# Issue in program order, with the stages written as a software pipeline, in a spectral filter and FFN kernel

## The chip, the cores and the metric

The kernel runs on one core of a Trainium2 chip. The metric is device time in microseconds, the median of three runs. The core has TensorE (PE, matmuls into PSUM), VectorE (DVE), ScalarE (ACT) and GpSimd (POOL) for elementwise work, and SyncE (SP), which issues the DMAs. Each engine takes its own instructions one after the other; semaphores make it wait for others.

## What is computed

```python
def reference(A_x, A_w_r, A_w_i, B_x, B_w1, B_b1, B_w2, B_b2):
    def _A_ref(x, w_r, w_i):
        B, S, D = x.shape
        X = (lambda x, axes=(-2,-1): jnp.fft.rfft2(x.astype(jnp.float32), axes=axes))(x, axes=(-2, -1))
        W = w_r + 1j * w_i
        X = X * W
        y = (lambda x, s, axes=(-2,-1): jnp.fft.irfft2(x, s=s, axes=axes).astype(jnp.bfloat16))(X, (S, D), axes=(-2, -1))
        return y
...
    x = A_x
    h = x + _A_ref(_layernorm(x, axis=-1), A_w_r, A_w_i)
    h2 = h + _B_ref(_layernorm(h, axis=-1), B_w1, B_b1, B_w2, B_b2)
    return h2
```

`x` is 2048 x 512 in bf16. The first half is a layernorm, a real 2-D FFT, a product with a complex filter, the inverse FFT and a residual. `_B_ref` is an FFN: 512 to 1792, the square of the ReLU, back to 512, with biases, on the layernorm of the result.

## The kernel before

The 2048 rows lie as 128 partitions of 16 groups `g`. Every FFT is written as matmuls with tables of sines, which the kernel makes itself: integer phases (`fiK`, `fiG`, `fiE`, `fiI`) on DVE or POOL, and the sine on ACT (`KF`, `GF`, `EF`, `GI`). `EI` and `KI` are transposes of EF and KF, made on PE and copied out by DVE.

The **front** loads `xs`, takes the statistics of each group (`bn_stats`, `bn_aggr` into `mv1`, then `rs1` on POOL), normalizes into `un`, and multiplies with KF (stage 1); ACT copies the result to `Bt`. Beside it the filter is scaled into `WB`: half of it straight on POOL, the reversed half through a matmul with a flip matrix `J` and a copy from PSUM (`pw`).

The **pair stage** is a loop `for pr in range(8)`. Stage 2 multiplies Bt by GF (8 matmuls of 256 columns, copy `U` on ACT). Stage 3 multiplies U by EF (4 of 512, copy `AB` on ACT, or `X` for pair 0). The spectral work on DVE makes `X` out of AB, the products `mA` and `mB` with WB, `Z` and `M`; POOL mends a few columns in `real_channels`. Stage 4 multiplies M by EI (8 of 256, copy into `T2` on ACT).

The **FFN part** works in chunks of four groups. `prep(c)` does stage 5 for each group (four matmuls of T2 with GI, copy `od` on ACT, sum and difference `R` on DVE), a matmul with KI, the residual `hs`, statistics, `hb` (hs with the last bias, on POOL), then `rs2`, the normalized `u2` and eight transposes twice into `UT`. `mlp(c)` does 14 times four matmuls of 512 columns with W1, a ReLU `rl` on ACT and its square `act` on DVE; then for each group 14 matmuls with W2 into `po`, the sum `ot` and the store.

The order of calls is `prep(0)`, `prep(1)`, `mlp(0)`, `prep(2)`, `mlp(1)`, `prep(3)`, `mlp(2)`, `mlp(3)`. The text does not fix the order in which an engine issues: the framework's scheduler orders each engine's instructions by its own priorities and cost figures, with the text's order as priority, and so mixes neighbouring steps where it finds them ready.

Of the kernel before, what the change touches and what calls it, by code (L numbers as in the profile page):

```python
# [19 lines left out]


@with_exitstack
def kernel(
# [127 lines left out]
    for c in range(4):  # L151
        for g in range(4 * c, 4 * c + 4):
# [3 lines left out]
        sl = slice(4 * c, 4 * c + 4)  # L156
        nc.gpsimd.tensor_scalar(rs1[:, sl], mv1[:, sl, 1], EPS, None, ALU.add)
        nc.gpsimd.tensor_tensor(rs1[:, sl], rs1[:, sl], mhalf[:], ALU.pow)  # L158
        for g in range(4 * c, 4 * c + 4):
            nc.vector.tensor_scalar(un[:, g, :], xs[:, g, :], mv1[:, g, 0:1], rs1[:, g:g + 1],  # L160
                                    ALU.subtract, ALU.mult)
        for h in range(2):
            pt = mm_tile("p1")
            pv = pt[:].rearrange("p (t e i c) -> p t e i c", t=2, e=2, i=2)
            g0 = 4 * c + 2 * h
            for t in range(2):
                for i in range(2):
                    g = g0 + i
                    o = pv[:, t, :, i, :]
                    nc.tensor.matmul(o, lhsT=un[:, g, P * t:P * t + P], rhs=KFlo, start=True, stop=False)  # L170
                    nc.tensor.matmul(o, lhsT=un[:, g, 256 + P * t:256 + P * t + P], rhs=KFhi, start=False, stop=True)
            dst = Bt[:].rearrange("p e q (g s) -> p e g q s", s=8)[:, :, g0:g0 + 2]
            nc.scalar.copy(dst, pt[:].rearrange("p (e i q s) -> p e i q s", e=4, i=2, q=16))

# [271 lines left out]
```

## Time and profile before

| | |
|---|---|
| median of three runs | 293.75 us (292.48 to 294.24) |
| profiled execution | 294.23 us |
| its span, first to last instruction | 292.4 us |
| mean granted TensorE clock | 0.784 |
| busy: PE, DVE, ACT, POOL | 180.6, 128.3, 93.0, 56.7 us |

The profile is one execution. Busy times are sums over the span; where engines take turns, no sum is near the span. The granted clock is 1.0 at the high level of 2.4 GHz and 0.5 at the low one of 1.2 GHz; a matmul's length follows it.

### The profile page before, as it was taken

What the parts mean: (1) busy time and instruction counts of PE and PEld (TensorE: products, weight loads), DVE (VectorE), ACT (ScalarE), POOL (GpSimd) and SP (SyncE); (2) the same over time, 40 slices, a digit from 0 to 9 for tenths busy, and PEclk for the clock granted to TensorE, in tenths of its full rate; (3) what the DMA queues carried; (4) which work ended last, traced back from release to release, by engine and by line L of the source; (5) the groups of instructions that cost most, each with busy time, mean ns of one, the idle gap of its engine ahead of it and who ended that gap; (6) DMA issues with size and microseconds to landing.
All of it is one profiled execution on the core that took longest, in us unless ns stands there. A gap on an engine that the chain in (4) does not pass through costs nothing.

```text
span 292.4 us, 2459 instructions
## 1 busy us (share of the span) xinstructions
PE 180.6 (62%) x858; PEld 93.2 (32%) x872; DVE 128.3 (44%) x299; ACT 93.0 (32%) x123; POOL 56.7 (19%) x109
## 2 busy tenths in 40 slices
PE   0066575363264245343536999329997449999995
PEld 0034364132133123121413444115443124444442
DVE  3795433224314413447572531753523744323421
ACT  1126661422341242121312830106700109505700
POOL 2776513101101110114332000340000430000000
PEclk9999576565775676555566999758999559999999
DMA  7994000000000000000000001000001000011011
GB/s 238 421 283 155 0 2 1 0 0 0 0 0 2 0 0 0 0 1 0 0 1 2 0 0 54 20 0 0 0 18 56 0 0 0 2 36 36 1 39 36
DMA packets 7469, 10.27 MB, mean 35 GB/s; under 512 B 2208, under 2 KB 6176, under 8 KB 7200
## 3 DMA queue, kind: packets, MB, share of 16 engines
q1 hardware_dynamic: 7456, 10.11, 10.2%
q8 instruction: 7, 0.11, 0.2%
q14 instruction: 6, 0.05, 0.1%
HBM read 8.01 MB, written 2.10 MB: 35 GB/s over the span
## 4 chain that ended last, share of the span: by engine, by line
PE 54%; DVE 26%; ACT 8%; POOL 5%; issue 3%; DMA 1%; POOLq 0%; ACTq 0%; DVEq 0%
PE ph L395 17%; PE po L403 16%; DVE hs L367 4%; PE p L251 3%; PE p L366 3%; DVE st L369 3%; DVE un L160 3%; ACT U L254 3%; DVE st L154 3%; PE p L385 3%; PE p L316 2%; ACT AB L277 2%; PE p L317 2%; DVE mA L288 2%; DVE R L363 2%
## 5 line engine op out<-in xcount | busy, mean ns | idle before, releaser
L395 PE MATMUL ph<-UT,W 128*128 128x512 bf16 x217 | 51.1, 387 | 0.3
L403 PE MATMUL po<-W,act 128*128 128x512 bf16 x220 | 48.8, 379 | 0.2
L397 ACT ACTIVATE rl<-ph,b1f 128x512 bf16<-128x512 f32 x56 | 37.2, 694 | 19.2 <-PE ph L395 18.8
L398 DVE TENSOR_TENSOR act<-rl 128x512 bf16<-128x512 bf16 x56 | 23.8, 425 | 33.0 <-ACT rl L397 33.0
L371 POOL TENSOR_TENSOR hb<-hs,b2b 128x512 f32<-128x512 bf16 x16 | 18.4, 1150 | 91.2 <-DVE hs L367 84.5
L316 PE MATMUL p<-EI,M 128*128 128x256 bf16 x28 | 11.6, 414 | 32.8 <-DVE M L300 32.8
L403 PEld LDWEIGHTS <-act 128*128 128x128 bf16 x224 | 22.0, 98 | 26.4
L395 PEld LDWEIGHTS <-W 128*128 128x128 bf16 x224 | 22.2, 100 | 24.7
L405 DVE TENSOR_TENSOR ot<-po,hb 128x512 bf16<-128x512 f32 x16 | 11.1, 692 | 35.5 <-PE po L403 35.5
L170 PE MATMUL p<-KF,un 128*128 128x256 bf16 x32 | 12.5, 395 | 20.1 <-DVE KF L127 14.2
L361 ACT COPY od<-p 128x256 f32<-128x256 f32 x16 | 6.0, 372 | 58.4 <-PE p L358 58.3
L282 DVE TENSOR_TENSOR X<-AB 128x512 bf16<-128x512 bf16 x7 | 3.0, 428 | 46.8 <-ACT AB L277 46.8
L366 PE MATMUL p<-R,KI 128*128 128x512 bf16 x16 | 8.9, 556 | 22.0 <-DVE R L364 22.0
L318 ACT CAST T<-p 128x1024 bf16<-128x1024 f32 x8 | 8.1, 1012 | 44.2 <-PE p L317 39.1
L385 PE MATMUL p<-ident,u 128*128 128x128 bf16 x64 | 9.5, 304 | 15.7 <-DVE u L378 15.2
L367 DVE TENSOR_TENSOR hs<-p,xs 128x512 bf16<-128x512 f32 x16 | 11.1, 692 | 10.4 <-PE p L366 10.4
L316 PEld LDWEIGHTS <-M 128*128 128x128 bf16 x28 | 3.6, 130 | 37.6 <-DVE M L300 36.7
L358 PE MATMUL p<-GI,T 128*128 128x256 bf16 x64 | 14.8, 373 | 1.1 <-ACT T L318 1.1
L386 ACT COPY UT<-p 128x1024 bf16<-128x1024 bf16 x8 | 7.7, 1015 | 24.2 <-PE p L385 24.2
L385 PEld LDWEIGHTS <-u 128*128 128x128 bf16 x64 | 7.3, 142 | 25.2 <-DVE u L378 22.4
L160 DVE TENSOR_SCALAR un<-xs,mv,rs 128x512 bf16<-128x512 bf16 x16 | 11.1, 742 | 4.7 <-POOL rs L158 4.7
L251 PE MATMUL p<-GF,Bt 128*128 128x256 bf16 x64 | 13.1, 370 | 0.0
(123 smaller groups left out, 241.2 us busy)
## 6 DMA issues: line engine op xcount, KB each, us to landing
W<-in_B_w_dram SPq DMA_DIRECT2D x2, 1792.0 KB, 12.7
xs<-in_A_x_dram SPq DMA_DIRECT2D x4, 512.0 KB, 5.6
out_dram<-ot SPq DMA_DIRECT2D x16, 128.0 KB, 1.8
Wn<-in_A_w_r_dram SPq DMA_DIRECT2D x1, 1028.0 KB, 9.1
Wn<-in_A_w_i_dram SPq DMA_DIRECT2D x1, 1028.0 KB, 10.8
b2b<-in_B_b_dram SPq DMA_DIRECT2D x1, 128.0 KB, 15.6
b1b<-in_B_b_dram SPq DMA_DIRECT2D x1, 3.5 KB, 15.9
```

The source lines that it names most:

```text
L160: nc.vector.tensor_scalar(un[:, g, :], xs[:, g, :], mv1[:, g, 0:1], rs1[:, g:g + 1], ALU.subtract, ALU.mult)
L251: nc.tensor.matmul(puv[:, q, :, e, :], lhsT=Bt[:, 2 * t + e, 2 * pr + q, :], rhs=GFv[:, t, :, e, :], start=(t == 0), stop=(t == 1))
L316: nc.tensor.matmul(o, lhsT=M[:, 0, r, c0:c0 + P], rhs=ei[:, P:3 * P], start=True, stop=False)
L358: nc.tensor.matmul(pe[:, 256 * e:256 * e + 256], lhsT=T2[:, lt, g].rearrange("p q s -> p (q s)"), rhs=GI[:, lt, :], start=(r == 0), stop=( ...
L366: nc.tensor.matmul(py[:], lhsT=KI[:], rhs=R[:], start=True, stop=True)
L367: nc.vector.tensor_tensor(hs[:, g, :], py[:], xs[:, g, :], ALU.add)
L371: nc.gpsimd.tensor_tensor(hb[:, g, :], hs[:, g, :], b2b[:], ALU.add)
L385: nc.tensor.transpose(pt[:, 512 * d + P * i:512 * d + P * i + P], u2[:, i, bass.ts(d2 + d, P)], ident[:])
L395: nc.tensor.matmul(ph[:], lhsT=W1[:, d, bass.ts(f, P)], rhs=UT[:, d, :], start=(d == 0), stop=(d == ND - 1))
L397: nc.scalar.activation(rl[:], ph[:], ACT.Relu, bias=b1f[:, f:f + 1], scale=1.0)
L398: nc.vector.tensor_tensor(act[:, f, :], rl[:], rl[:], ALU.mult)
L403: nc.tensor.matmul(po[:], lhsT=act[:, f, bass.ts(i, P)], rhs=W2[:, f, :], start=(f == 0), stop=(f == NF - 1))
```

## The change

Every engine's instructions are tied, each to the one before it, so that the engine issues in the order of the text (`pin`), and the text is written anew.

- In the front all phase tables come first, fiG on DVE instead of POOL. `xs` comes in five pieces. EF's third kind and EI's are negations of the first on DVE, so that 19 blocks are transposed instead of 28. Five of sixteen `un` go to ACT, two of the four WB copies to DVE. W2 is loaded ahead of the two biases.
- The pair loop is skewed: in one turn stage 4 of pair `pr - 1`, stage 3 of `pr + 1`, stage 2 of `pr + 2` and the spectral work of `pr`. U and AB have three buffers instead of two. The last T2 copy is split between ACT and DVE.
- The FFN works in chunks of 2, 2, 4, 4 and 4 groups. The next chunk's preparation is a list of steps (`prep_steps`, some of them empty), which `run` hands out between the slots of the current chunk: a slot is one W1 group, or some five W2 matmuls. `hb` follows `rs2` on POOL; half of the `u2` go to ACT and half of the UT copies to DVE. PSUM is split into three banks for preparation, three for `ph` and two for `po`.

```diff
+def pin(tc, nc):
+
+    last = {}
+    for ins in list(nc.cur_bb.bb.instructions):
+        prev = last.get(ins.engine)
+        if prev is not None:
+            tc.add_manual_dep(ins, prev.name,
+                              mybir.DependencyInfo(mybir.DependencyClass.NoSync, mybir.DependencyReason.DATA),
+                              reason="program order")
+        last[ins.engine] = ins
...
+    CH = ((0, 2), (2, 4), (4, 8), (8, 12), (12, 16))
+    for a, b in CH:
+        nc.sync.dma_start(xs[:, a:b, :], xv[:, a:b, :])
...
     nc.sync.dma_start(W1[:], B_w1.rearrange("(c p) f -> p c f", p=P))
+    nc.sync.dma_start(W2[:], B_w2.rearrange("(i p) d -> p i d", p=P))
     nc.sync.dma_start(b1b[:], B_b1.rearrange("(i p) -> p i", p=P))
     nc.sync.dma_start(b2b[:], B_b2.unsqueeze(0).to_broadcast([P, D]))
-    nc.sync.dma_start(W2[:], B_w2.rearrange("(i p) d -> p i d", p=P))
...
+        nc.vector.tensor_scalar(fiG[:, o:o + 257], idxL[:, 0:257], cols[:, t:t + 1], float(QT), ALU.mult, ALU.add)
...
+    for i, off in ((0, 0), (1, QT)):
+        nc.gpsimd.tensor_scalar(fiE[i][:], idxK[:], cols[:, 3:4], float(off), ALU.mult, ALU.add)
+        nc.scalar.activation(
+            EF[:, :, i, :], fiE[i][:].bitcast(I16)[:, ::2].rearrange("p (a b) -> p a b", a=9), ACT.Sin,
+            scale=SIN_SCALE)
...
+    ON_ACT = (3, 7, 11, 13, 15)
...
+    ln1_stats(0, 2)
+    nc.vector.tensor_scalar(EF[:, :, 2, :], EF[:, :, 0, :], -1.0, None, ALU.mult)
...
+    ln1_norm(12, 16)
+    stage1(12)
+    stage1(14)
+    w_direct((1, 4))
+    w_direct((4, 8))
+    nc.vector.tensor_copy(EI[:, 0:8, 0:2, :], tr[:].rearrange("p (a k b) -> p a k b", a=8, k=2))
+    nc.vector.tensor_copy(EI[:, 8, 0:2, :], tr2[:, 0:2 * P].rearrange("p (k b) -> p k b", k=2))
+    nc.vector.tensor_copy(KI[:], tr2[:, 2 * P:3 * P])
+    nc.vector.tensor_scalar(EI[:, :, 2, :], EI[:, :, 0, :], -1.0, None, ALU.mult)
...
+                if k0 == 1:
+                    nc.vector.tensor_scalar(WB[i][:, k0:k0 + nk, 1, :], src, WSC, None, ALU.mult)
+                else:
+                    nc.scalar.activation(WB[i][:, k0:k0 + nk, 1, :], src, ACT.Copy, scale=WSC)
...
+        if split:
+            nc.scalar.copy(dst[:, :, :, 0:8], src[:, :, :, 0:8])
+            nc.vector.tensor_copy(dst[:, :, :, 8:16], src[:, :, :, 8:16])
+        else:
+            nc.scalar.copy(dst, src)
...
+    stage2(0)
+    stage2(1)
+    stage3(0)
+    w_reversed()
+    w_real()
+    stage3(1)
+    stage2(2)
+    spectral(0)
+    for pr in range(1, 9):
+        stage4(pr - 1, split=(pr == 8))
+        if pr + 1 < 8:
+            stage3(pr + 1)
+        if pr + 2 < 8:
+            stage2(pr + 2)
+        if pr < 8:
+            spectral(pr)
+        if pr == 4:
+            sin_of(GI[:].rearrange("p t c -> p (t c)"), fiI[:])
+            nc.gpsimd.memset(GI[0:1, 2, 0::2], 1.0)
+            nc.gpsimd.memset(GI[0:1, 2, 1::2], -1.0)
+            nc.gpsimd.tensor_copy(b1f[:], b1b[:])
...
+    def rstd(a, b):
+        nc.gpsimd.tensor_scalar(rs2[:, a:b], mv2[:, a:b, 1], EPS, None, ALU.add)
+        nc.gpsimd.tensor_tensor(rs2[:, a:b], rs2[:, a:b], mhalf[:, 0:b - a], ALU.pow)
+        for g in range(a, b):
             nc.gpsimd.tensor_tensor(hb[:, g, :], hs[:, g, :], b2b[:], ALU.add)
...
+    CHUNKS = ((0, 2), (2, 4), (4, 8), (8, 12), (12, 16))
...
+        if half == 0:
+            nc.scalar.copy(dst, src)
+        else:
+            nc.vector.tensor_copy(dst, src)
...
+    def prep_steps(c):
+
+        a, b = CHUNKS[c]
+        steps = []
+        for g in range(a, b):
+            steps.append((lambda g=g: s5(g)))
+            steps.append(None)
+            if g > a:
+                steps.append((lambda g=g - 1: s6(g)))
+        steps.append(None)
+        steps.append((lambda g=b - 1: s6(g)))
+        steps.append((lambda: rstd(a, b)))
+        steps.append(None)
+        steps.append(None)
+        steps.append((lambda: norm(c, True)))
+        steps.append(None)
+        steps.append((lambda: transp(c, 0)))
+        steps.append((lambda: transp(c, 1)))
+        return steps
...
-    prep(0)
-    prep(1)
-    mlp(0)
-    prep(2)
-    mlp(1)
-    prep(3)
-    mlp(2)
-    mlp(3)
+            slots.append(lambda f=f: up(f))
+        for i in range(b - a):
+            for f0, f1 in ((0, 5), (5, 10), (10, NF)):
+                slots.append(lambda i=i, f0=f0, f1=f1: down(i, f0, f1))
+        return slots
...
+    def run(c, prep, delay=0):
+
+        slots = mlp_slots(c)
+        n = len(slots)
+        done = 0
+        for k, slot in enumerate(slots):
+            slot()
+            want = (len(prep) * (k + 1) + n - 1) // n if k < n - 1 else len(prep)
+            while done < want:
+                if prep[done] is not None:
+                    prep[done]()
+                done += 1
+
+    for g in range(0, 2):
+        s5(g)
+    for g in range(0, 2):
+        s6(g)
+    rstd(0, 2)
+    norm(0, True)
+    transp(0, 0)
+    transp(0, 1)
+    for c in range(5):
+        run(c, prep_steps(c + 1) if c + 1 < 5 else [])
+    pin(tc, nc)
```

What the changed order looks like at three places, first before and then after.

DVE in the front, where the tables KF and fiG stand between the statistics of layernorm 1 (`st`, `mv1`):

```order
L154 BN_STATS st_182<-xs_58 128x6
L121 SCALAR_TENSOR_TENSOR fiK_116<-rowA_102,pF_113,offA_106 128x128
L124 TENSOR_SCALAR mask_118<-subc_104,pF_113 128x128
L131 TENSOR_SCALAR cols_115<-pF_113 128x1
L132 TENSOR_SCALAR cols_115<-pF_113 128x1
L155 BN_AGGR mv1_85<-st_182 128x2
L154 BN_STATS st_185<-xs_58 128x6
L154 BN_STATS st_214<-xs_58 128x6
L160 TENSOR_SCALAR un_83<-xs_58,mv1_85,rs1_86 128x512
L127 TENSOR_TENSOR KF_79<-kft_120,mask_118 128x128
L160 TENSOR_SCALAR un_83<-xs_58,mv1_85,rs1_86 128x512
L128 TENSOR_SCALAR KF_79<-KF_79 128x128
```

After, on the same engine, from the last fiG steps on:

```order
L165 TENSOR_SCALAR fiG_115<-idxL_110,cols_113 128x255
L164 TENSOR_SCALAR fiG_115<-idxL_110,cols_113 128x257
L165 TENSOR_SCALAR fiG_115<-idxL_110,cols_113 128x255
L169 TENSOR_TENSOR KF_79<-kft_120,mask_119 128x128
L170 TENSOR_SCALAR KF_79<-KF_79 128x128
L185 BN_STATS st_154<-xs_58 128x6
L186 BN_AGGR mv1_85<-st_154 128x2
L185 BN_STATS st_157<-xs_58 128x6
L186 BN_AGGR mv1_85<-st_157 128x2
L228 TENSOR_SCALAR EF_81<-EF_81 128x9x128
L185 BN_STATS st_164<-xs_58 128x6
```

The two KF steps stood among the `un`; now they, and the fiG steps that were on POOL, stand ahead of the first statistics.

ACT in the middle of the pair stage, the copies out of PSUM (p2 is stage 2, p3 stage 3, p4 stage 4):

```order
L318 CAST T2_68<-p4_532 128x4x2x16x8
L254 CAST U_551<-p2_542 128x1024
L277 CAST AB_559<-p3_553 128x1024
L318 CAST T2_68<-p4_579 128x4x2x16x8
L254 CAST U_598<-p2_589 128x1024
L277 CAST AB_606<-p3_600 128x1024
```

After, two turns of the new loop on ACT:

```order
L408 CAST T2_68<-p4_568 128x4x2x16x8
L352 CAST AB_583<-p3_578 128x1024
L327 CAST U_594<-p2_585 128x1024
L408 CAST T2_68<-p4_615 128x4x2x16x8
L352 CAST AB_630<-p3_625 128x1024
L327 CAST U_641<-p2_632 128x1024
```

Before, T2, U and AB follow one another around one pair: the U copy (p2_542) is what the next AB is made from. After, the three copies of one turn belong to three pairs, and the U copy is read by stage 3 of the next turn.

ACT at a chunk edge of the FFN (`od` and UT are preparation, `rl` is the FFN):

```order
L397 ACTIVATE rl_1089<-ph_1084,b1f_61 128x512
L397 ACTIVATE rl_1097<-ph_1092,b1f_61 128x512
L397 ACTIVATE rl_1105<-ph_1100,b1f_61 128x512
L361 COPY od_1185<-p5_1180 128x256
L361 COPY od_1202<-p5_1197 128x256
L361 COPY od_1219<-p5_1214 128x256
L361 COPY od_1236<-p5_1231 128x256
L386 COPY UT_1255<-p7_1256 128x1024
L386 COPY UT_1255<-p7_1266 128x1024
L397 ACTIVATE rl_1282<-ph_1277,b1f_61 128x512
L397 ACTIVATE rl_1290<-ph_1285,b1f_61 128x512
```

After, on ACT, the edge of the same chunk and what follows it:

```order
L487 ACTIVATE u2_1259<-hs_798,nm2_802,rs2_801 128x512 x2
L506 COPY UT_1276<-p7_1277 128x1024
L543 ACTIVATE rl_1310<-ph_1305,b1f_61 128x512
L458 COPY od_1318<-p5_1313 128x256
L543 ACTIVATE rl_1328<-ph_1323,b1f_61 128x512
L543 ACTIVATE rl_1336<-ph_1331,b1f_61 128x512
L458 COPY od_1344<-p5_1339 128x256
L543 ACTIVATE rl_1354<-ph_1349,b1f_61 128x512
L543 ACTIVATE rl_1362<-ph_1357,b1f_61 128x512
L543 ACTIVATE rl_1370<-ph_1365,b1f_61 128x512
```

The four `od` and two UT stood in one block between two chunks' `rl`; now the `od` stand between the `rl` of the chunk before, and one UT copy is left on ACT.

## Rows read from the trace of the kernel before

**Rows 1.** The page: span, busy share of TensorE, and its granted clock in 40 slices.
```profile
span 292.4 us, 2459 instructions
...
PE 180.6 (62%) x858; PEld 93.2 (32%) x872; DVE 128.3 (44%) x299; ACT 93.0 (32%) x123; POOL 56.7 (19%) x109
...
PEclk9999576565775676555566999758999559999999
```

**Rows 2.** Table by stage: length, busy time of each engine, granted clock, DMA.
```profile
0.00:46.49 46.49, 20.80 (x123) 13.79 (x124) 25.84 (x69) 20.24 (x21) 23.02 (x51) 0.89 0.51 173
46.49:125.13 78.64, 34.27 (x155) 19.46 (x157) 27.52 (x62) 22.17 (x22) 10.34 (x34) 0.63 0.00 0
125.13:156.57 31.44, 13.38 (x59) 7.07 (x60) 19.53 (x47) 4.91 (x10) 11.71 (x12) 0.55 0.00 1
156.57:182.76 26.19, 25.86 (x125) 12.58 (x128) 8.55 (x19) 11.01 (x16) 0.00 (x0) 0.95 0.05 16
182.76:197.52 14.76, 5.17 (x24) 2.19 (x22) 10.20 (x24) 1.49 (x4) 5.83 (x6) 0.62 0.03 10
...
241.20:288.88 47.68, 47.43 (x216) 21.42 (x219) 16.75 (x35) 20.20 (x30) 0.00 (x0) 1.00 0.06 20
```

**Rows 3.** Chain of waits through one pair: start, length, what.
```profile
70.50 0.40 PE p L316
...
72.52 1.51 PE p L251 x8
...
74.10 1.02 ACT U L254
...
76.36 1.02 ACT AB L277
...
80.91 0.39 PE p L316
```

**Rows 4.** The same table for three stretches of one pair.
```profile
59.80:63.10 3.30, 3.27 (x15) 2.20 (x16) 0.31 (x1) 1.01 (x1) 0.45 (x2) 0.50 0.00 0
63.10:65.80 2.70, 1.42 (x6) 0.44 (x4) 0.00 (x0) 1.04 (x2) 0.00 (x0) 0.94 0.00 0
65.80:70.50 4.70, 0.00 (x0) 0.00 (x0) 3.32 (x8) 0.98 (x1) 0.53 (x2) 0.61 0.00 0
```

**Rows 5.** Groups by line: count, busy, mean ns, idle before.
```profile
L398 DVE TENSOR_TENSOR act<-rl 128x512 bf16<-128x512 bf16 x56 | 23.8, 425 | 33.0 <-ACT rl L397 33.0
...
L154 DVE BATCH_NORM_STATS2 st<-xs 128x6 f32<-128x512 bf16 x16 | 10.3, 666 | 5.0 <-DMA xs<-in_A_x_dram 5.0
```

**Rows 6.** Timeline of DVE and POOL while `un` is written.
```profile
18.73 3.02 DVE L160 TENSOR_SCALAR un<-xs,mv,rs 128x512 bf16<-128x512 bf16 x4
...
19.07 1.90 POOL L209 TENSOR_SCALAR WB<-Wn 128x2048 bf16<-128x2048 bf16 x1
...
23.76 1.38 DVE L160 TENSOR_SCALAR un<-xs,mv,rs 128x512 bf16<-128x512 bf16 x4
```

**Rows 7.** Chain of waits at the end of the front.
```profile
26.97 1.23 POOL fiE L183
28.20 1.01 POOL rs L158
...
29.24 1.34 DVE un L160
...
40.05 3.34 ACT WB L222 x4
```

**Rows 8.** Chain of waits at the end of `prep(2)`.
```profile
193.39 0.70 DVE hs L367
...
194.16 1.15 POOL hb L371
...
195.58 1.05 POOL rs L374
```

**Rows 9.** Waits over the span: total, times, longest.
```profile
PE p L366 <- DVE R L364: 22.0, 15, 1.8
```

More of the change, by code (lines that the diff above doesn't have):

```diff
@@ L155 @@
             nc.vector.bn_aggr(mv1[:, g, :], st[:])
[L156 to L165, printed above, removed]
-            for t in range(2):
[L167 to L173, printed above, removed]
@@ new lines, in stage1 @@
+    def stage1(g0):
+        pt = mm_tile("p1")
+        pv = pt[:].rearrange("p (t e i c) -> p t e i c", t=2, e=2, i=2)
+        for i in range(2):
+            for t in range(2):
+                g = g0 + i
+                o = pv[:, t, :, i, :]
+                nc.tensor.matmul(o, lhsT=un[:, g, P * t:P * t + P], rhs=KFlo, start=True, stop=False)
+                nc.tensor.matmul(o, lhsT=un[:, g, 256 + P * t:256 + P * t + P], rhs=KFhi, start=False, stop=True)
+        dst = Bt[:].rearrange("p e q (g s) -> p e g q s", s=8)[:, :, g0:g0 + 2]
+        nc.scalar.copy(dst, pt[:].rearrange("p (e i q s) -> p e i q s", e=4, i=2, q=16))
@@ L243, with stage2 @@
     GFv = GF[:].rearrange("p t (r e j) -> p t r e j", r=2, e=2)
-    for pr in range(8):
+    Us, Xs, ABs, BSs, Zs, Ms = {}, {}, {}, {}, {}, {}
+    def stage2(pr):
         pu = mm_tile("p2")
@@ L389, in mlp, with bank, s5 @@
-    def mlp(c):
+    nm2 = ffn.tile([P, G], FP32, name="nm2")
+    def bank(name, tag, bufs, dt=FP32):
+        return ps.tile([P, 2048 // mybir.dt.size(dt)], dt, tag=tag, name=name, bufs=bufs)
+    Rs = {}
+    def s5(g):
+        pe = bank("p5", "pp", 3)
+        for e in range(2):
+            for r in range(2):
+                lt = 2 * r + e
+                nc.tensor.matmul(pe[:, 256 * e:256 * e + 256], lhsT=T2[:, lt, g].rearrange("p q s -> p (q s)"),
+                                 rhs=GI[:, lt, :], start=(r == 0), stop=(r == 1))
+        od = ffn.tile([P, 256], FP32, tag="od", bufs=2, name="od")
+        nc.scalar.copy(od[:], pe[:, 256:512])
+        Rs[g] = R = ffn.tile([P, 512], BF16, tag="R", bufs=3, name="R")
+        nc.vector.tensor_tensor(R[:, 0:256], pe[:, 0:256], od[:], ALU.add)
+        nc.vector.tensor_tensor(R[:, 256:512], pe[:, 0:256], od[:], ALU.subtract)
@@ L390, in mlp, with mlp_slots @@
+    def mlp_slots(c):
+        a, b = CHUNKS[c]
+        n = P * (b - a)
         UT = UTs[c]
         act = ffn.tile([P, NF, 512], BF16, tag="act", bufs=2, name="act")
-        for f in range(NF):
-            ph = bank("ph")
-            for d in range(ND):
-                nc.tensor.matmul(ph[:], lhsT=W1[:, d, bass.ts(f, P)], rhs=UT[:, d, :], start=(d == 0), stop=(d == ND - 1))
-            rl = ffn.tile([P, 512], BF16, tag="rl", bufs=3, name="rl")
-            nc.scalar.activation(rl[:], ph[:], ACT.Relu, bias=b1f[:, f:f + 1], scale=1.0)
-            nc.vector.tensor_tensor(act[:, f, :], rl[:], rl[:], ALU.mult)
@@ L413, with up @@
-    prep(3)
-    mlp(2)
-    mlp(3)
+        slots = []
+        def up(f):
+            ph = bank("ph", "ph", 3)
+            for d in range(ND):
+                nc.tensor.matmul(ph[:, 0:n], lhsT=W1[:, d, bass.ts(f, P)], rhs=UT[:, d, 0:n],
+                                 start=(d == 0), stop=(d == ND - 1))
+            rl = ffn.tile([P, 512], BF16, tag="rl", bufs=3, name="rl")
+            nc.scalar.activation(rl[:, 0:n], ph[:, 0:n], ACT.Relu, bias=b1f[:, f:f + 1], scale=1.0)
+            nc.vector.tensor_tensor(act[:, f, 0:n], rl[:, 0:n], rl[:, 0:n], ALU.mult)
@@ new lines, in mlp_slots, with down @@
+        state = {}
+        def down(i, f0, f1):
+            if f0 == 0:
+                state[i] = bank("po", "po", 2)
+            po = state[i]
+            for f in range(f0, f1):
+                nc.tensor.matmul(po[:], lhsT=act[:, f, bass.ts(i, P)], rhs=W2[:, f, :], start=(f == 0), stop=(f == NF - 1))
+            if f1 == NF:
+                g = a + i
+                ot = ffn.tile([P, D], BF16, tag="ot", bufs=3, name="ot")
+                nc.vector.tensor_tensor(ot[:], po[:], hb[:, g, :], ALU.add)
+                nc.sync.dma_start(ov[:, g, :], ot[:])
```

319 lines of the change are left out of this document (170 added, 149 removed).

## The prediction

> **What bounds the kernel now.** I read the page first: TensorE is busy 62% of 292.4 us, and the strip of granted clock stands at 5 to 7 tenths from a tenth of the span to half of it, and again twice later [rows 1]. So no engine is the bound; something makes them take turns. The table by stage says where [rows 2]. I cut the span at the first spectral product (46.49), the first inverse row matmul of `prep` (125.13), the first FFN matmul (156.57) and the edges of the later `prep`s. The front takes 46.49 us, the eight-pair stage 78.64 us with PE at 34.27 and DVE at 27.52 busy, the entry into the FFN 31.44 us. `mlp(0)` runs at full PE (25.86 of 26.19), then `prep(2)` opens a hole of 14.76 us with PE busy 5.17; `prep(3)` opens another, and the last two `mlp` calls run without a hole: 47.68 us, 23.84 each. PE is the limit only inside `mlp`.
>
> In the pair stage the chain of waits shows the turns [rows 3]: stage 4 from 70.50, stage 2 from 72.52, the U copy at 74.10, stage 3, the AB copy at 76.36, then the spectral work on DVE to the M that lets the next stage 4 start at 80.91. That is 10.41 us a pair, the sum of the three engines' shares and not the largest of them: stage 2 of a pair stands behind stage 4 of the pair before it, and each copy waits for its matmuls.
>
> **The change, part by part.** The sum is made on the profiled execution: 294.23 us with a span of 292.4, so 1.8 us lie outside. The median of the three runs is 293.75, 0.2% lower, which changes nothing below. A measurement of this kernel can tell about 1% from no change.
>
> *Pair stage.* DVE per pair: from the end of AB (77.38) to the stage 4 that its first M releases (80.91) 3.53 us [rows 3], and a second M of some 0.3, so 3.8. ACT: three copies of 1.02, 3.1. PE: at the low clock fifteen 256-column matmuls took 3.27 us (0.50 granted [rows 4]), 0.218 each; a pair has 8 + 8 of them and four of 512 columns, 24 in that unit: 5.2 us, and 2.6 at the high clock. The new order issues stage 4 of pair k-1, stage 3 of k+1 and stage 2 of k+2 while DVE does pair k. What loops is: end of spectral k-1, stage 4 (0.9 at the high clock), T copy 1.02, AB copy 1.02, some 0.2 of handing over, spectral k+1: 3.1 us, inside the 3.8 that spectral k takes. So DVE is the bound at the high clock: 2.6 for pair 0 (no X) + 7 x 3.8 = 29.2. At the low clock the same loop is PE's 5.2.
>
> Which clock? In the stretch after the burst PE was busy 1.42 of 2.70 us, with the wait for U in it, at 0.94 granted; in the next 4.70 us it did nothing and the mean fell to 0.61 [rows 4]. The new loop keeps PE busy 2.6 of 3.8 us with holes of about one U copy. I take the high clock, after one turn at the low one (PE waits for pair 0's spectral work first): +1.4. The last stage 4 and the copy of T, cut in halves for ACT and DVE, add 0.9 to 1.7 and 0.5: +1.8. Pair stage 32.4 us; bounds 30 and 38.
>
> *Front.* Removed: one of three sine tables for EF (now a negation), 9 of 28 transposes, five of sixteen `un` on DVE (to ACT), two of four WB copies on ACT (to DVE). The tables come first on DVE and POOL, the chunks of `xs` are smaller at the start. DVE's queue to the last `un`: tables some 4 us from 1.0 (the same kinds of small instructions as before, with fiG's four moved here), then sixteen statistics at 0.67 [rows 5] = 10.7, eleven `un` at 0.35 (1.38 for four [rows 6]) = 3.8, EF's negation and waits for the sine and for POOL's `rs` some 2: the last `un` at 21.5 to 23. Before, the last group of `un` only began at 29.24, behind `rs`, which stood behind an EF table on POOL [rows 7]. After the last `un`: stage 1 of its pair 1.7 (low clock), Bt copy 1.0, stage 2 of pair 0 1.7, U 1.0, stage 3 some 1.7, pw matmuls 1: 31. DVE then has two WB copies of 1024 columns from PSUM; ACT took 3.34 for all four [rows 7], a DVE copy from PSUM is not shown at this width, so between 0.8 each and 1.3 (the 512-column `ot` and `hs` kind took 0.70 [rows 8], doubled and less an overhead). 2.4 for both: 33.4.
>
> POOL works beside this. Four `un` took 3.02 us while POOL scaled WB, and 1.38 when it did not [rows 6]. The new WB scaling begins beside the last chunk's `un` and the negation of EI, so I add 1.6, that pair's difference: 35.0. The Trainium skill (SBUF — State Buffer, Who interferes with whom) says that one of the two engines fully waits while the other holds a port pair that they share. By it the price could also fall on POOL, and the front would then keep 33.4. Bounds for the front: 31 (no contention, high clock early) and 40 (two such collisions and a late sine).
>
> `rs` of the last chunk now stands behind two WB scalings on POOL that wait for Wn. Wn was in use at 19.07 in the trace [rows 6], and this `rs` is needed at about 20, so it costs nothing; if Wn came later, it would delay the front one for one. On SP the W2 load now goes ahead of the two bias loads: their first readers come after 50 us, and before the change all loads were done when the pair stage began (DMA share 0.00 in the second row of [rows 2]).
>
> *Entry to the FFN.* Two groups instead of eight stand ahead of the first FFN matmul. From the last T: stage 5 twice 1.0, `od` 0.4, the two R 0.8, KI matmul 0.5, then DVE's 0.7 + 0.7 + 0.1 twice with little between = 3.0, `rs` 1.05 and a short step ahead of it, 1.3 [rows 8], `u2` 0.6, transposes and UT 1.7. 9.3 us against 31.44; bounds 8.5 and 11. `rs` no longer queues behind `hb` (1.15 [rows 8]), which now follows it.
>
> *FFN.* PE's own work: 4 x 23.84 = 95.4. The other fourteen groups' preparation is 4 x 256 + 512 + 4 x 128 = 2048 columns each, four 512-column matmuls of 0.213 (23.84 / 112): 14 x 0.85 = 11.9. Together 107.3, in place of the 132.3 from 156.57 to 288.88. What hides the rest: per chunk of four groups DVE has 10.2 for preparation (one `ot` in it) and 16.75 / 2 for the FFN [rows 2], 18.6 of 27.2 us; ACT 1.5 + 10.1. If that cover were gone, PE would wait as before, below. Three places lack it. The clock starts low: +1.7. The second chunk has two groups of FFN (15.3 us of PE with the preparation of four), and its first half has DVE at 9.5 + 14 x 0.25 (act at half the width, from 0.43 [rows 5]) = 13.0 against PE's 6 + 2.6: some 3.5 lost, since `act` is squared in the queue behind `hs` and statistics. Chunk edges, where `u2` meets `hb` on POOL: 0.5 each, 2 in all. FFN 114.5; bounds 110 and 122.
>
> *Sum:* 35.0 + 32.4 + 9.3 + 114.5 + 3.5 (last `ot` and store, unchanged) = 194.7; with 1.8: 196.5, so **197 us**. All low ends give 185, all high ends 216.
>
> **The rivals.** *The clock does not hold in the pair stage.* For it: the loop leaves PE a hole every pair, and the trace never shows 2.6 of 3.8 us for long. Against: 1.42 of 2.70 held. Then the loop is PE's 5.2: 7 x 1.4 = 9.8 more, 206. The Trainium skill has this as a rule of its own (TensorE: Matmul & The Clock Gate, A second HAM failure mode: psum-queue depth-cycling): short idle times between groups of matmuls that cycle through PSUM banks make the clock swing between its levels. By that rule it is this rival's 206; the trace so far does not bear it out.
>
> *Preparation stalls the FFN's queue.* PE is in order, so an FFN slot behind a KI matmul waits for R. Before, these waits were 22.0 us for 15, 1.47 each [rows 9]. Against: a slot of 0.85 and more now stands between stage 5 and the KI matmul. If it all comes back, 14 x 1.47 = 20.6: 217.
>
> *Slower than before.* If those holes also keep the clock at its low level through the FFN, PE's 107.3 become 215 and the total 304. It decides from a mean granted clock of 0.52: 97 us lost on 107.3. Against: `mlp` has 0.95 and 1.00 [rows 2], and preparation fills holes with matmuls.
>
> *The order is not the program's.* The built order follows the new text on every engine, so this is out.
>
> **How the numbers follow.** Forecast 0.70, clock rival 0.15, stalls 0.12, slower 0.03. The range is 185 to 217: it holds the forecast with its bounds, the clock rival and about half of the stalls. Faster by over 1% 0.96, within 1% 0.01, slower 0.03.
>
> **What would show it.** First spectral product at 33 to 37; pairs some 3.8 us apart with DVE the releaser of stage 4 and the clock near 1.0; first FFN matmul at 74 to 80; from there PE busy over 90%, with its longest waits in the second chunk; all waits of the KI matmul for R below 5 us. A pair period of 5 with a clock near 0.5, or KI waits near 20 us, would make it wrong.

## The result and the profile after

The changed kernel takes 202.0 us (median of four runs, 201.91 to 204.29) against 294.0 us in the same series: 0.689 of the time, 95% interval 0.684 to 0.695. A second series of six runs gave 202.5 us and 0.691 (0.687 to 0.695); runs that differ by 1% are compared with that one. Single runs of the changed kernel lie in two groups, 201.5 to 202.1 and 203.3 to 204.4 us, so a median can move by 1 to 2 us with their number, and a difference of that size is taken here only where the stages of the profile show it too. The forecast was 197 in 185 to 217. The profiled execution took 202.05 us, its span is 200.3, so 1.75 lie outside.

The page of the changed kernel, in the parts that answer to [rows 1]: span, TensorE's busy share, its busy tenths and its granted clock in 40 slices of 5 us.

```profile
span 200.3 us, 2641 instructions
...
PE 157.7 (79%) x919; PEld 88.8 (44%) x919; DVE 140.2 (70%) x320; ACT 98.5 (49%) x144; POOL 56.2 (28%) x113
...
PE   0046959499774450999997699999999999999992
...
PEclk9999999958999655699999999999999999999999
```

TensorE has 158 busy us where it had 181: nearly the same products (nine transposes fewer), fewer of them at the low clock. The strip stands below 9 only in slices 9 and 10, and 14 to 17: two places, and both come up below. In its first slices the strip can't be read as the clock: it has 9 from the start, but up to 21.8 us the 256-column matmuls start 0.21 us apart, as at the low level, and 0.11 us apart only from 22.9 us on. The front's 1.00 below, and its 0.89 in [rows 2], hold such a stretch too.

The table by stage answers to [rows 2]. The cuts are the first spectral product, the first stage 5, the first FFN matmul, points near the starts of the second and third chunk (96.57 and 116.36), the last FFN matmul. Columns as there: PE, weight loads, DVE, ACT, POOL, clock, DMA.

```profile
0.00:35.34 35.34, 18.07 (x129) 12.75 (x130) 26.58 (x73) 20.79 (x23) 21.84 (x50) 1.00 0.67 227
35.34:69.88 34.54, 23.92 (x145) 14.37 (x143) 27.97 (x64) 20.95 (x23) 10.40 (x37) 0.85 0.00 1
69.88:80.96 11.08, 4.09 (x18) 2.12 (x18) 7.00 (x13) 2.14 (x4) 3.19 (x4) 0.50 0.00 0
80.96:96.73 15.77, 15.64 (x104) 10.35 (x104) 11.21 (x29) 8.30 (x18) 3.39 (x4) 0.92 0.03 10
96.73:116.00 19.27, 15.82 (x115) 10.41 (x113) 16.59 (x39) 9.98 (x21) 5.80 (x6) 1.00 0.04 14
116.00:196.80 80.80, 80.21 (x417) 38.81 (x415) 50.14 (x103) 36.28 (x57) 11.53 (x12) 1.00 0.06 20
196.80:200.30 3.50, 0.00 (x0) 0.00 (x0) 0.69 (x1) 0.00 (x0) 0.00 (x0) 0.91 0.11 37
```

The pair stage is 34.54 us with DVE busy 27.97, where it was 78.64 with DVE at 27.52: the same work on DVE, with 6.6 us of gaps instead of 51. The entry fell from 31.44 to 11.08. Of the 92.1 us by which the span is shorter, 11.2 are in the front, 44.1 in the pair stage, 20.4 in the entry and 16.5 in the FFN. The FFN has one stretch that loses time, the second chunk with 19.27 - 15.82 = 3.45 us; the last three chunks lose 0.59 in 80.80. TensorE's waits in that chunk (start, length, what; in brackets the wait ahead of it and what ended it):

```profile
105.86 0.38 PE L465 MATMUL p<-R,KI 128*128 128x512 bf16 x1 [1.05 <-DVE R L461]
...
109.91 2.55 PE L553 MATMUL po<-W,act 128*128 128x512 bf16 x11 [0.43 <-DVE act L544]
113.55 0.28 PE L502 MATMUL p<-ident,u 128*128 128x128 bf16 x2 [1.09 <-DVE u L490]
114.70 0.51 PE L502 MATMUL p<-ident,u 128*128 128x128 bf16 x6 [0.87 <-DVE u L490]
```

The timeline of DVE, of each X of pairs 2 to 5, with its wait and what ended it:

```profile
43.86 0.45 DVE L362 TENSOR_TENSOR X<-AB 128x512 bf16<-128x512 bf16 x1 [2.23 <-ACT AB L352]
...
48.12 0.42 DVE L362 TENSOR_TENSOR X<-AB 128x512 bf16<-128x512 bf16 x1 [0.35 <-ACT AB L352]
...
51.81 0.42 DVE L362 TENSOR_TENSOR X<-AB 128x512 bf16<-128x512 bf16 x1
...
55.52 0.42 DVE L362 TENSOR_TENSOR X<-AB 128x512 bf16<-128x512 bf16 x1
```

From pair 3 on the pairs are 3.7 us apart, and from pair 4 on DVE waits for no AB; before, a pair took 10.41. The stretches below are a turn in which TensorE is slow, and two later ones:

```profile
41.00:46.20 5.20, 5.20 (x21) 3.02 (x20) 2.80 (x7) 3.08 (x4) 0.99 (x4) 0.51 0.00 0
46.20:55.00 8.80, 7.42 (x52) 4.70 (x50) 7.91 (x19) 7.71 (x9) 2.28 (x8) 1.00 0.01 2
55.00:66.00 11.00, 6.26 (x40) 3.54 (x40) 10.40 (x25) 7.58 (x8) 3.96 (x15) 1.00 0.00 1
```

At 41 to 46 TensorE is busy all the time at 0.51, and DVE waits. Ahead of it TensorE had waited 1.17 us for the Z that POOL writes for pair 0 (stage 4 of pair 0), and stage 3 of pair 2 stands behind that:

```profile
40.13 0.29 PE L395 MATMUL p<-EI,Z 128*128 128x128 bf16 x1 [1.17 <-POOL Z L312]
...
40.79 0.63 PE L347 MATMUL p<-U,EF 128*128 128x512 bf16 x1
```

Later it is busy 6.26 of 11.00 us and keeps 1.00.

The timeline at the entry, behind the last statistics of DVE:

```profile
76.52 0.73 POOL L473 TENSOR_TENSOR rs<-rs,mhalf 128x2 f32<-128x2 f32 x1
77.22 2.26 POOL L475 TENSOR_TENSOR hb<-hs,b2b 128x512 f32<-128x512 bf16 x2
77.28 1.10 DVE L484 SCALAR_TENSOR_TENSOR nm<-mv,rs 128x2 f32<-128x2 f32 x1 [1.27 <-POOL rs L473]
78.30 1.32 DVE L490 TENSOR_SCALAR u<-hs,mv,rs 128x512 bf16<-128x512 bf16 x1
...
79.68 1.03 PE L502 MATMUL p<-ident,u 128*128 128x128 bf16 x8 [6.07 <-DVE u L490]
```

`nm` has two columns and takes 1.10 us; `u2` takes 1.32. Both lie beside `hb` on POOL, and TensorE waits 6.07 us for them and what is ahead of them. The waits of the KI matmul for R, 22.0 us before [rows 9], are the second line here (total, times, longest):

```profile
PE p L502 <- DVE u L490: 8.0, 3, 6.1
...
PE p L465 <- DVE R L461: 1.7, 3, 1.1
```

### The profile page after: what moved, and what is told of

It is laid out like the page before. It is cut to its first block, busy times and chain, and to the rows that moved or that the text cites. A ratio compares the mean times of both kernels' runs of the same rounds, so it can differ in the third digit from the quotient of the medians.

```text
span 200.3 us, 2641 instructions
## 1 busy us (share of the span) xinstructions
PE 157.7 (79%) x919; PEld 88.8 (44%) x919; DVE 140.2 (70%) x320; ACT 98.5 (49%) x144; POOL 56.2 (28%) x113
## 4 chain that ended last, share of the span: by engine, by line
PE 58%; DVE 30%; ACT 6%; POOL 3%; issue 2%; DVEq 0%; POOLq 0%; ACTq 0%
PE ph L540 22%; PE po L553 22%; DVE st L185 4%; PE p L455 4%; DVE st L468 2%; DVE mA L369 2%; ACT Bt L212 2%; DVE u L490 2%; DVE mB L369 2%; DVE hs L466 2%; PE p L502 2%; PE p L324 1%; DVE Z L371 1%; PE p L209 1%; DVE act L544 1%
## 5 line engine op out<-in xcount | busy, mean ns | idle before, releaser
L540 PE MATMUL ph<-UT,W 128*128 128x512 bf16 (+1 forms) x280 | 54.5, 341 | 0.9 <-DVE UT L508 0.5
L543 ACT ACTIVATE rl<-ph,b1f 128x512 bf16<-128x512 f32 (+1 forms) x70 | 41.5, 602 | 23.0 <-PE ph L540 20.1
L540 PEld LDWEIGHTS <-W 128*128 128x128 bf16 x280 | 27.8, 99 | 23.0 <-issue 2.7
L544 DVE TENSOR_TENSOR act<-rl 128x512 bf16<-128x512 bf16 (+1 forms) x70 | 24.8, 365 | 16.6 <-ACT rl L543 15.8
L209 PE MATMUL p<-KF,un 128*128 128x256 bf16 x32 | 10.3, 343 | 15.8 <-DVE un L199 14.7
L487 ACT ACTIVATE u<-hs,nm,rs 128x512 bf16<-128x512 bf16 x8 | 6.2, 808 | 27.3 <-DVE nm L484 27.3
L212 ACT CAST Bt<-p 128x1024 bf16<-128x1024 f32 x8 | 7.9, 1014 | 7.8 <-PE p L210 7.8
L468 DVE BATCH_NORM_STATS2 st<-hs 128x6 f32<-128x512 bf16 x16 | 11.1, 695 | 0.6
L185 DVE BATCH_NORM_STATS2 st<-xs 128x6 f32<-128x512 bf16 x16 | 10.7, 668 | 0.0
L210 PE MATMUL p<-KF,un 128*128 128x256 bf16 x32 | 10.4, 346 | 0.0
L490 DVE TENSOR_SCALAR u<-hs,mv,rs 128x512 bf16<-128x512 bf16 x8 | 10.1, 1289 | 0.0
```

Of the source, the lines that this page charges most:

```text
L468: nc.vector.bn_stats(st[:], hs[:, g, :])
L490: nc.vector.tensor_scalar(u2[:, g - a, :], hs[:, g, :], mv2[:, g, 0:1], rs2[:, g:g + 1], ALU.subtract, ALU.mult)
L540: nc.tensor.matmul(ph[:, 0:n], lhsT=W1[:, d, bass.ts(f, P)], rhs=UT[:, d, 0:n], start=(d == 0), stop=(d == ND - 1))
L543: nc.scalar.activation(rl[:, 0:n], ph[:, 0:n], ACT.Relu, bias=b1f[:, f:f + 1], scale=1.0)
L544: nc.vector.tensor_tensor(act[:, f, 0:n], rl[:, 0:n], rl[:, 0:n], ALU.mult)
```

## Experiments

Each is an edit of the changed kernel unless said otherwise. Ratios are to the kernel before, with their 95% intervals; stage times are of the profiled execution.

**Is it the holding of the order, or the order of the text?**

```diff
@@ end of the kernel function @@
-    pin(tc, nc)
```

> The new text, but without the call that holds every engine to the program's order, so the scheduler orders each engine as it did in the kernel before. Theory A (the order is what pays): the scheduler pulls the stages of a pair together again and puts a chunk's preparation in one piece; 250 to 290 us, with pairs some 10 us apart and holes of 10 us and more between the chunks of the FFN. Theory B (the rewritten text pays, and the scheduler keeps most of its order): 202 to 215 us. In between, the trace says which stage falls back.

Measured: 200.66 us, 0.682 (0.676 to 0.688), no slower than with `pin`. The scheduler kept the pairs 3.7 to 4.2 us apart, by the X in the timeline of DVE:

```profile
49.90 0.42 DVE L362 TENSOR_TENSOR X<-AB 128x512 bf16<-128x512 bf16 x1
...
53.60 0.42 DVE L362 TENSOR_TENSOR X<-AB 128x512 bf16<-128x512 bf16 x1
...
57.80 0.42 DVE L362 TENSOR_TENSOR X<-AB 128x512 bf16<-128x512 bf16 x1 [0.40 <-ACT AB L352]
```

It moved little: first spectral product 38.94 instead of 35.34 (tables and `un` in another order), and at the entry it put `hb` ahead of `rs`, where `nm` takes 0.16 and `u2` 0.41. From the first stage 5 to the end it is 3.6 us shorter, which gives the front's 3.6 back. Theory A is false; theory B's kind holds, a little below its 202 us.

The other half of the comparison is the old text, with the function `pin` called at its end:

```diff
@@ the kernel before, end of the kernel function @@
     mlp(2)
     mlp(3)
+    pin(tc, nc)
```

> The text of the kernel before, with the call that holds every engine to the program's order added and nothing else. Theory A (holding the order is worth nothing by itself, the rewritten order is all): not faster than the kernel before, 290 to 330 us; slower where the scheduler had interleaved the groups of a preparation. Rival (the scheduler's choices cost the kernel before its time): 205 to 270.

Measured: 306.37 us, 1.043 (1.039 to 1.048), as theory A has it: holding the old order costs 4%. Its waits:

```profile
PE p L328 <- DVE M L312: 32.8, 7, 4.8
PE p L378 <- DVE R L376: 24.5, 16, 1.9
```

So the gain is in the text as it is written anew; holding its order gives nothing here, and did harm to the old text, which takes turns. The new text changes more than the order: it also gives work to other engines, leaves out nine transposes and a sine table, and cuts the chunks and PSUM otherwise. The two experiments that follow take back the order alone, in the pair stage and in the FFN. The 11.2 us of the front are not taken apart by any run, so which of its edits brought them is not shown.

**The skew.**

```diff
-    stage2(0)
-    stage2(1)
-    stage3(0)
     w_reversed()
     w_real()
...
-    for pr in range(1, 9):
-        stage4(pr - 1, split=(pr == 8))
...
+    for pr in range(8):
+        stage2(pr)
+        stage3(pr)
+        spectral(pr)
+        stage4(pr, split=(pr == 7))
```

> Order held, but stages 2, 3, spectral and 4 of a pair are issued in a row, pair by pair, with the four WB copies ahead of them. Theory A (the skew sets the pair stage): a pair takes the sum of its engines' shares again, 10.4 us as in the kernel before, against 3.71 now; 7 x 6.7 = 47 us more, so 245 to 255 us, with the clock near 0.5 in this stage. Rival (DVE is the bound whatever the order is, since pools let PE run ahead): the pairs stay 3.7 to 5 us apart and the time is 202 to 212 us.

Measured: 249.04 us, 0.848 (0.843 to 0.854), as theory A has it. First spectral product to first stage 5, and two X in the timeline of DVE:

```profile
34.37:117.67 83.30, 38.17 (x155) 20.39 (x158) 28.33 (x63) 22.68 (x23) 10.66 (x39) 0.57 0.00 0
```

```profile
66.66 0.42 DVE L362 TENSOR_TENSOR X<-AB 128x512 bf16<-128x512 bf16 x1 [6.67 <-ACT AB L352]
...
77.14 0.43 DVE L362 TENSOR_TENSOR X<-AB 128x512 bf16<-128x512 bf16 x1 [6.70 <-ACT AB L352]
```

A pair takes 10.48 us, the clock is 0.57, and the stage 83.30 instead of 34.54. The 48.8 us are all of the loss (46.5 by the medians).

**Preparation between slots.**

```diff
@@ def run(c, prep, delay=0) @@
+        for step in prep:
+            if step is not None:
+                step()
+        prep = []
...
-            want = (len(prep) * (k + 1) + n - 1) // n if k < n - 1 else len(prep)
-            while done < want:
...
```

> Order held, but the preparation of the next chunk is issued in one piece ahead of the FFN slots of the chunk before it, and not between them. Theory A (preparation between slots is what keeps PE busy): four holes come back. The kernel before had 14.76 us with PE at 5.17 busy for four groups, so 9.6 lost; three such and half of one for the chunk of two groups, 3.5 x 9.6 = 34, less the 3.5 that the second chunk loses now: 232 us (220 to 245). Rival (PE would be kept busy anyway, since the preparation of one chunk can wait on ACT and DVE while PE runs ahead): within 5 us of 202.

Measured: 249.54 us, 0.851 (0.846 to 0.856). The kind is theory A's, the size is not: 47 us lost, not 30. Its waits:

```profile
PE p L502 <- DVE u L490: 33.6, 8, 6.5
...
PE p L465 <- DVE R L461: 12.2, 13, 1.8
```

These two are 45.8 us where the changed kernel has 9.7, so the holes cost 36. The other 10 are TensorE's own, in the table by stage from 80.64 us on, where the second chunk's preparation has just begun:

```profile
80.64:246.00 165.36, 121.89 (x619) 63.02 (x627) 82.84 (x172) 55.55 (x95) 20.59 (x22) 0.86 0.04 13
```

It is busy 121.89 us at a mean clock of 0.86, against 15.64 + 15.82 + 80.21 = 111.67 in the changed kernel, whose clock there is 0.92 and then 1.00. I had counted the holes, too small, and left out that work behind a hole runs at the low clock.

**The slow turn.** A call moves in the first turn only:

```diff
     for pr in range(1, 9):
-        stage4(pr - 1, split=(pr == 8))
+        if pr > 1:
+            stage4(pr - 1, split=(pr == 8))
         if pr + 1 < 8:
             stage3(pr + 1)
         if pr + 2 < 8:
             stage2(pr + 2)
+        if pr == 1:
+            stage4(0)
```

> In the first turn of the pair stage alone, stage 3 of pair 2 and stage 2 of pair 3 are issued ahead of stage 4 of pair 0 and not behind it. Theory A (TensorE's hole there, while it waits for pair 0's Z, cost the clock and made DVE wait 2.23 + 0.35 us for AB): X of pair 2 follows M of pair 1 at once and the clock holds; 2 to 2.6 us less, 199.5 to 200. Rival (the clock falls at this place whatever is issued there, and the wait comes back at pair 3): the pair stage stays at 34.5 us and the time within 0.5 us of 202.

Measured: 199.78 us, 0.682 (0.679 to 0.685). X of pair 2 starts at once, the stage 3 that it needs starts at 37.23 and not 40.79, and the same stretch 41 to 46.2 has the high clock:

```profile
37.23 0.38 PE L347 MATMUL p<-U,EF 128*128 128x512 bf16 x1 [1.14 <-ACT U L327]
...
41.39 0.42 DVE L362 TENSOR_TENSOR X<-AB 128x512 bf16<-128x512 bf16 x1
```

```profile
41.00:46.20 5.20, 4.05 (x28) 2.67 (x30) 4.87 (x13) 3.48 (x4) 2.11 (x8) 1.00 0.00 0
```

The pair stage falls from 34.54 to 31.79, by 2.75: theory A, a little over its size. The run does not part the clock from the place in the queue, since the moved call changes both. An estimate from the rows: the four matmuls of that stage 3 took 1.71 us at the low level (40.79 to 42.50) and take 0.86 here, so some 0.85 of the 2.23 us of waiting was the clock, and the rest was standing behind a stage 4 that waited for Z.

**`hb` and the normalization.** First I issued `hb` behind the transposes:

```diff
 def rstd(a, b):
-        for g in range(a, b):
-            nc.gpsimd.tensor_tensor(hb[:, g, :], hs[:, g, :], b2b[:], ALU.add)
...
         steps.append((lambda: transp(c, 0)))
-        steps.append((lambda: transp(c, 1)))
+        steps.append((lambda: (transp(c, 1), bias2(a, b))))
```

> The addition of the bias into hb on POOL (two of 2.26 us at the entry) is issued after the transposes of its chunk and not ahead of the normalization. Theory A (hb and DVE hold each other up): at the entry nm falls from 1.10 us to some 0.2 and u2 from 1.3 to 0.4, 1.8 to 2.2 us; at the edge of the second chunk two u2 of 2.48 in all fall to 0.8, 1.5 to 2 more; the later chunks' u2 are hidden. 198 to 199 us. Rival (the small operation is slow for another reason, or hb only moves its collision onto the UT copy on DVE): 201 to 203 us.

Measured: 202.99 us, 0.694 (0.688 to 0.700), and `nm` is 1.10 again: POOL has nothing else to do behind `rs`, so `hb` started at 76.84, right beside `nm`, whatever stood between them in the text. The run decides nothing about the theory. Then `hb` right behind its group's `hs`, which puts it ahead of `rs` in POOL's queue:

```diff
 def s6(g):
         nc.vector.tensor_tensor(hs[:, g, :], py[:], xs[:, g, :], ALU.add)
+        nc.gpsimd.tensor_tensor(hb[:, g, :], hs[:, g, :], b2b[:], ALU.add)
...
 def rstd(a, b):
-        for g in range(a, b):
-            nc.gpsimd.tensor_tensor(hb[:, g, :], hs[:, g, :], b2b[:], ALU.add)
```

> The bias addition into hb on POOL is issued right behind each group's hs, so that it runs beside the statistics of DVE and ahead of rs, not beside nm and u2. Theory A (hb beside nm and u2 is what makes them slow): nm falls from 1.10 to some 0.16 and u2 from 1.3 to 0.42 at the entry, 1.8 to 2 us less there; at the edge of the second chunk 1 to 1.6 less: 198.5 to 199.5. Rival 1 (hb now holds up hs and the statistics by as much): 201.5 to 202.5. Rival 2 (rs waits for hb on POOL): 202 to 204.

Measured: 200.25 us, 0.685 (0.682 to 0.687). The timeline at the entry:

```profile
77.11 0.16 DVE L483 SCALAR_TENSOR_TENSOR nm<-mv,rs 128x2 f32<-128x2 f32 x1 [1.44 <-POOL rs L474]
77.19 0.41 DVE L489 TENSOR_SCALAR u<-hs,mv,rs 128x512 bf16<-128x512 bf16 x1
77.30 0.81 ACT L486 ACTIVATE u<-hs,nm,rs 128x512 bf16<-128x512 bf16 x1 [5.49 <-DVE nm L483]
```

`nm` and `u2` are short, as theory A says, 1.85 us less from the start of `nm` to the end of `u2`. The entry gains only 1.28 of them (first stage 5 to first FFN matmul 9.80, before 11.08): ACT's own `u2` ends at 78.11 and is late next, and `rs` starts a little later. The median gains 2.2 us (202.5 to 200.25), the span of the profiled execution 1.9. That lies between theory A's 198.5 to 199.5 and rival 1's 201.5: the statistics are not held up, but `act` is. At half width it takes up to 0.52 us beside the moved `hb`, where it took 0.26, and in the second chunk two waits of TensorE grow, from 1.05 and 0.43 us, while those for `u2` shrink from 1.96 to 0.23:

```profile
105.40 0.38 PE L465 MATMUL p<-R,KI 128*128 128x512 bf16 x1 [1.57 <-DVE R L461]
...
109.97 2.55 PE L552 MATMUL po<-W,act 128*128 128x512 bf16 x11 [0.95 <-DVE act L543]
```

**The low clock between the pair stage and the FFN.**

```diff
+    def keep(n):
+        pd = mm_tile("pd")
+        for _ in range(n):
+            nc.tensor.matmul(pd[:, 0:512], lhsT=J[:], rhs=W1[:, 0, 0:512], start=True, stop=True)
...
+        if pr > 6:
+            keep(10 if pr == 7 else 6)
         if pr < 8:
             spectral(pr)
...
+    keep2(24)
     rstd(0, 2)
```

> Forty matmuls of 512 columns whose result nobody reads are added where TensorE waits at the end of the pair stage: ten ahead of the last stage 4, six behind it, twenty-four behind the second KI matmul. Theory A (what the low clock costs from 66.5 to 83 us is the time of the work there): stage 4 of the last pair 1.78 to 0.95, stage 5 and KI some 0.8 less, transposes 0.4 less, the first chunk of the FFN 1.3 less: 3 to 3.5 us less, 198.5 to 199. Rival (these matmuls delay what stands behind them, or the clock does not rise in time): no gain, 201.5 to 203, with the entry still at a clock near 0.5.

Measured: 199.1 us, 0.678 (0.675 to 0.680). From the last M over the entry into the first chunk:

```profile
66.30:69.15 2.85, 2.52 (x15) 1.32 (x16) 1.05 (x3) 0.59 (x1) 0.45 (x2) 1.00 0.00 0
69.15:79.45 10.30, 7.54 (x41) 3.64 (x43) 7.10 (x13) 2.15 (x4) 3.20 (x4) 1.00 0.00 0
```

The clock is 1.00 where it was 0.50 to 0.52. Stage 4 with the copy of T is 2.85 against 3.48, the entry 10.30 against 11.08, and the second chunk starts 14.33 us behind the first FFN matmul where it was 15.61. These are 2.7 us by the stages, a little under theory A's 3 to 3.5, and 3.4 by the medians.

**The size of the first chunks.**

```diff
-    CHUNKS = ((0, 2), (2, 4), (4, 8), (8, 12), (12, 16))
+    CHUNKS = ((0, 4), (4, 8), (8, 12), (12, 16))
...
```

The entry changes with it: the KI matmul of a group is issued behind the stage 5 of the next one.

> Four chunks of four groups and not five of which the first two have two groups, so that four groups are prepared ahead of the first FFN matmul and no chunk of two has to cover the preparation of four. Theory A (the second chunk's 3.45 us are lost because its cover is half as long): those 3.45 are given back, but two more groups at the entry cost DVE 2 x 2.4 and the clock stays low for longer: 203 to 205. Rival (the loss in the second chunk comes from the half-width act, whatever stands beside it, or the entry hides the two groups): 198.5 to 201.

Measured: 201.83 us, 0.688 (0.685 to 0.691): no difference that can be told, and between the ranges of theory A and the rival.

```profile
70.19:87.73 17.54, 7.33 (x36) 4.20 (x36) 12.38 (x24) 4.02 (x7) 5.81 (x6) 0.60 0.00 0
87.73:197.80 110.07, 108.69 (x545) 52.88 (x555) 70.37 (x145) 49.35 (x77) 17.31 (x18) 0.98 0.06 19
```

The entry costs 6.5 more and the FFN 5.8 less (115.84 to 110.07). Of the 5.8, 2.8 are waits (4.17 to 1.38 us) and 3.0 are work of TensorE: the theory had the waits about right and forgot that two groups' preparation, 1.7, leaves the FFN.

**All edits that paid.** The moved call, `hb` behind `hs`, the added matmuls (14 for the 24), and `split=False`.

> The three edits of the runs before together (stage 3 of pair 2 first, extra matmuls where TensorE waits, fourteen and not twenty-four of them at the entry, hb behind hs), and the last T copy whole on ACT. Theory A (they remove different waits): their gains against 202.0 add up, 2.2 + 2.9 + 1.8 and 0.3 for the copy: 195 (194 to 196.5). Rival (the extra matmuls and hb early remove the same waits at the entry): 196.5 to 198.

Measured: 194.88 us, 0.664 (0.661 to 0.667), 3.8% below the changed kernel and inside theory A's range. The pair stage with its last copy and the entry:

```profile
34.80:67.41 32.61, 25.06 (x165) 14.88 (x167) 28.72 (x64) 22.82 (x24) 10.55 (x39) 1.00 0.00 1
67.41:76.74 9.33, 5.98 (x32) 3.03 (x32) 5.04 (x13) 2.09 (x4) 3.26 (x4) 0.94 0.00 0
```

With the halves, stage 5 started 1.40 us behind the end of the last stage 4: the halves ran one behind the other in the trace (DVE's waited 2.39 us, for ACT's). Here it starts 1.35 behind it, right at the end of the added matmuls, while the whole copy ends at 67.11 (66.10 + 1.01), 1.05 behind stage 4:

```profile
65.90 1.46 PE L390 MATMUL pd<-W,J 128*128 128x512 bf16 x5
67.41 1.03 PE L470 MATMUL p<-GI,T 128*128 128x256 bf16 x8
```

So cutting the copy bought nothing; the whole one was done 0.3 us earlier, and the added matmuls then took that up.

The same without the call of `pin`:

> The kernel with all four edits, without the call that holds the program's order. Theory A (as for the changed kernel, holding the order is worth nothing where the text is in a good order): within 2 us of 194.9. Rival (matmuls that nobody reads have no reader to hold them in place, so the scheduler moves them to where they delay others or keep no clock, and stage 3 of pair 2 goes back behind): 198 to 205.

Measured: 194.25 us, 0.664 (0.661 to 0.666), as with it.

The base of these comparisons is the changed kernel timed again:

> The changed kernel itself, timed in five rounds, so that the runs that differ from it by one per cent have a base with as narrow an interval: 202 us, ratio to the kernel before 0.686 to 0.690.

Measured: 202.5 us, 0.691 (0.687 to 0.695).

## Why the prediction was right, and where its sizes were off

The time is 202.0 where 197 was forecast, inside the range. By the steps of the sum, on the span of 200.3 against 194.7:

- *Front*, 35.0 forecast, 35.34 measured. The sum is near by luck, since its parts differ and cancel. The 1.6 of contention, counted at the last `un` and EI's negation, hardly show there (the last two `un` on DVE took 0.93, the negation 0.48). DVE's tables last until 6.91 us and not 5 (`mask` 1.24, two of `fiG` 1.18 and 1.23, KF 1.16, beside POOL's `idxK` and `fiE`). Stage 1 waits 1.03 for an `un` that ACT writes behind two Bt copies, a wait that the sum does not have. And the last stage 1, stage 2 and stage 3 ran at the high level, where the low one was counted. The two WB copies took 2.36, as forecast. What removing DVE's collision with POOL in the tables would give was not tried.
- *Pair stage*, 32.4 forecast, 34.54 measured. DVE as the bound with 3.8 a pair: 3.7, right; undoing the skew shows that it is the cause. The slow turn cost 2.6 in DVE's waits (2.23 + 0.35), 1.4 forecast. Stage 4 of the last pair and the copies took 3.40 from 66.48, where 1.8 was counted: the low clock for all of stage 4, and halves that ran in a row.
- *Entry*, 9.3 forecast, 11.08 measured. The terms as they are listed make 10.3 and not 9.3 (9.3 has one of the two stage 5), so the forecast by its own terms was 198. The step that failed is `u2` at 0.6: `nm` and `u2` took 2.34 beside `hb`, 1.7 more. The prediction put the meeting with `hb` at 0.5 at each chunk edge and at nothing here, since `rs` no longer queues behind it; but what stands behind `rs` on POOL runs beside what `rs` releases on DVE. Moving `hb` shows it. Some 1.1 come back elsewhere: 2.98 up to the first `hs` instead of 3.7, and 1.34 for the transposes and UT instead of 1.7.
- *FFN*, 114.5 forecast, 115.84 measured. Waits 4.2 against 5.5: the second chunk lost 3.45 as forecast, but not all for the reason given. The KI matmul and `act` have 1.05 + 0.43; the rest is its edge, where TensorE waits for `u2`, which runs beside `hb` (1.09 + 0.87). A UT copy that stands behind an `ot` (0.50) is most of the 0.59 after it; the later edges are hidden. Work 111.67 against 109.0; where the 2.7 lie was not followed up.
- The tail, 3.5, and 1.75 outside the span were right.

Of the signs named with the forecast one was missed, by the pair stage and the entry: the first FFN matmul is at 80.96 and not at 74 to 80. The others came: first spectral product 35.34, pairs 3.7 apart, TensorE busy 96% of the FFN, its waits in the second chunk, 1.7 us for R.

The rivals: the clock held in the pair stage from 46 to 66 us, at 1.00 from 55 to 66 us with TensorE busy 6.26 of 11.00 us and a hole in each pair. The rule of the Trainium skill (TensorE: Matmul & The Clock Gate, A second HAM failure mode: psum-queue depth-cycling) that short idle times between such groups of matmuls make the clock swing is not borne out by this trace there. The clock did fall twice in this stage: in the first turn, behind waits of 0.90, 0.44 and 1.17 us, and at the last stage 4, behind one of 2.44. Stalls of the FFN's queue for R: 1.7 us and not 20.6; with preparation in one piece 12.2 of them come back. *The order is not the program's* was put out because the built order follows the text; true, but the scheduler keeps the pairs 3.7 to 4.2 us apart without being held. The forecast credited nothing to holding the order by itself, and that stands.

## What to carry to other kernels

Where a stage takes the sum of its engines' shares, write its calls skewed, so that in each turn an engine that waits has the next pair's work ahead of it; whether the order was then held by force mattered little here, and holding the old order, which takes turns, cost 4%. At the first and the last turn of such a pipeline look again: each of the waits left there was some 1 to 3 us, and some also cost the clock. Work that nothing waits for soon still has a place: behind `rs` on POOL, `hb` made `nm` and `u2` 1.85 us longer at the entry; ahead of it, it left them alone and made `act` longer in the FFN, for a median gain of 2.2 us.

## What the hardware showed that I had not expected

- An operation of two columns on DVE takes 1.10 us beside POOL's 128x512 addition and 0.16 when that addition is over. The Trainium skill (SBUF — State Buffer, Who interferes with whom) says that one of the two engines waits fully while the other holds a port pair that they share; the trace agrees, for so small an operation too. DVE's statistics beside the same addition kept their 0.69 us or less.
- Forty matmuls without a use made the kernel 3.4 us faster in the median: TensorE stayed at the upper of its levels (1.2 and 2.4 GHz), granted 1.00, through 10.3 us in which it otherwise ran at 0.50.
- A hole of 1.17 us ahead of the slow turn, after two others of 0.90 and 0.44, came with a fall from 1.00 to 0.50; holes of 0.71 and 1.58 us at 59 to 63 us did not, nor did holes of 1.14, 0.30, 0.61 and 0.80 us between 36 and 45 us where the call of stage 4 was moved. Which of the holes brought the fall is not settled here.
